# Seven unread matrix products fewer ahead of one k-v product, and GpSimd's gain product in two halves

## The chip, the core and the metric

The kernel runs on one core of one Trainium2 chip. The core has five engines with a queue each: PE (TensorE, matrix products; PEld is its weight load), DVE (VectorE), ACT (ScalarE), POOL (GpSimd) and SP (SyncE, which here only issues DMAs). The metric is the device time of one execution in microseconds (us); lower is better.

## The reference

There are eight batches, eight heads, 576 positions of 64 channels each. For each batch and head `kv = k^T v` (64x64), then `raw = q kv`, and each row of `raw` is divided by its root mean square and multiplied by `g_norm`. The heads side by side give `x`, 576x512 for each batch. Then

```
theta = x @ w_theta
y = w_tok_r @ (x * cos(theta)) + w_tok_i @ (x * sin(theta))    # mixes the 576 positions
u = x + y
out = u + max(u @ w_ch, 0)
```

## The kernel before, in words

**Tiling.** A batch's 576 positions are four tiles of 128 rows (j = 0 to 3, 512 columns: "full") and one rest of 64 rows, kept as a 128x256 tile (j = 4; its names carry an "e"). `g_norm` is folded into the weights, so the kernel's `x` and `u` are without it, and it comes back at the end as `ug = u * g`.

**The stages of a tile**, with the lines of the profile: `kv` on PE (L244, fp32, 80 small products a batch, copied to `kbd`); q turned, by PE in the first two batches and by DMA transposes from batch 2 on (L296); `raw` on PE (L309, L318); its squares on ACT (L331), their sums on DVE (L340), the power -1/2 on POOL (`rt`, L347), `x` on DVE (L372, L381); `x` turned by PE (L264) and copied out by ACT (`xT`, L280); `th` on PE (L402, L407); its whole turns (`pt`, ACT L420), the rest (`arg`, DVE L426) and its absolute value (DVE L434); sine and cosine (ACT L442, L449); `zm`, x times both (DVE L462; `zf` for the rest tile, which SP then moves to `zt` in four DMAs, L470); `y` on PE (L485, L489); `u` (DVE L496); `u` turned (PE L264, ACT L280), `v` on PE (L402, L407); `ug = u * g` on POOL (L525); `ot = max(v, 0) + ug` (DVE L535); the store (SP, L544, L549).

**Loads.** k and v of a batch (`kt`, `vt`, two buffers) are loaded by SP (L185, L189), q by POOL (L195, L202). `w_ch` is loaded once, by SP (L632), and scaled by ACT into `wch` (four instructions, L565).

**What sets the order.** Nothing is scheduled by the machine. Tasks are numbered as they are made, and a list in the source, `TURNS`, written out by hand, gives the order in which they are issued; each engine takes its own in that order and waits in place where an input is missing. An entry `~n@ring` is no task: it takes a slot of a PSUM ring (`acc` has 4, `raw` 2) and issues n products of the identity with a tile of ones into it (`idle`, L589, 128x512 fp16). Nothing reads them; they only fill PE's time. There are 64 such products, all in the first 40 us. `~9@acc` stands directly ahead of the k-v product of batch 1, which is 80 products (L244).

**POOL's queue** holds, besides the q loads, the 36 `rt` and the 40 `ug`. `ug` has two buffers for full tiles and two for rest tiles.

Of the kernel before, what the change touches and what calls it, by code (L numbers as in the profile page):

```python
# [13 lines left out]
ALU = mybir.AluOpType  # L14
# [24 lines left out]
44 120 38 47 129 104 121 105 107 130 39 ~2@acc 122 111 42 138 40 48 123 131 139 124 41 171 132 53  # L39
125 140 172 126 49 133 127 147 167 134 50 148 128 135 112 ~2@acc 181 51 141 168 113 149 136 142 52  # L40
182 183 115 114 54 150 156 184 144 143 ~1@acc 179 55 151 157 145 173 180 56 250 177 146 174 158 116
178 137 175 159 57 169 176 160 117 161 162 163 170 118 164 152 153 165 ~9@acc 255 119 154 256 251
# [70 lines left out]
def kernel(  # L113
# [12 lines left out]
    nc = tc.nc  # L126
    B, H, S, D = q.shape
    C = H * D
    P = 128
# [44 lines left out]
    g8 = const.tile([P, D], FP32, name="g8")  # L174
# [19 lines left out]
    def load_q(b, hs):  # L194
        nc.gpsimd.dma_start(  # L195
            out=qh[b % NB][:, hs, :],
            in_=q[b, hs, 0:SM, :].rearrange("h (p j) d -> p h (j d)", j=NJ),
        )

    def load_qe(b):  # L200
        for hh in range(2):
            nc.gpsimd.dma_start(  # L202
                out=qe[b % NB][hh * TL:(hh + 1) * TL, :, :],
                in_=q[b, hh * HH:(hh + 1) * HH, SM:S, :].rearrange("h s d -> s h d"),
            )
# [24 lines left out]
    def full(j):  # L230
        return j < NJ

    raw_ps, th_ps, y_ps, v_ps, kv_ps, tr_ps = {}, {}, {}, {}, {}, {}
    qT, x_sb, x_pair, sq_sb, rt_sb, xT, pt_sb, arg_sb, sc_sb, zf_sb, u_sb, ug_sb, uT, ot_sb = (
        {}, {}, {}, {}, {}, {}, {}, {}, {}, {}, {}, {}, {}, {})
# [286 lines left out]
    def u_gain(b, j):  # L522
        h, w, e = (H, C, "") if full(j) else (HH, HC, "e")
        ug = work.tile([P, w], FP32, tag="ug" + e, bufs=2, name="ug")
        nc.gpsimd.tensor_tensor(  # L525
            out=ug[:].rearrange("p (h e) -> p h e", h=h),
            in0=u_sb[b, j][:].rearrange("p (h e) -> p h e", h=h),
            in1=g8[:].unsqueeze(1).broadcast_to((P, h, D)), op=ALU.mult,
        )
        ug_sb[b, j] = ug  # L530

    def finish(b, j):
# [64 lines left out]
    def add(kind, eng, cost, fn, deps=(), pos=0.0, takes=(), tail=0.0, shape=None):  # L597
        t = Task(kind, eng, cost, fn, [d for d in deps if d is not None], pos,
                 [ring(*r) for r in takes], tail + (0.06 if eng == "PE" else 0.0), shape)
        tasks.append(t)  # L600
        return t
# [18 lines left out]
    def load(queue, cost, mbytes, fn, deps=(), pos=0.0, kind="load"):  # L620
        return transfer(kind, queue, cost, mbytes * MB, fn, deps, pos)
# [15 lines left out]
    pool, h = load("POOL", 1.0, 0.52, lambda: load_q(0, slice(0, HH)), [pool], -50)  # L637
    q_got[0, 0] = [h]
    pool, h = load("POOL", 1.0, 0.52, lambda: load_q(0, slice(HH, H)), [pool], -47.5)
    q_got[0, 1] = [h]  # L640
    pool, h = load("POOL", 1.3, 0.14, lambda: load_qe(0), [pool], -46)
# [44 lines left out]
    for kc in range(NKC):  # L686
        e = "DVE" if kc % 2 else "ACT"
# [14 lines left out]
    for b in range(B):  # L702
# [22 lines left out]
        for j in (0, 2, 1, 3, 4) if b == 0 else range(NT):  # L725
# [4 lines left out]
            if b < QD:  # L730
# [3 lines left out]
                e = "ACT" if b or a else "DVE"  # L734
# [79 lines left out]
        for j in range(NT):  # L814
# [28 lines left out]
            else:  # L843
# [7 lines left out]
                     [uo, *channel_ready], s, [PS_ACC], shape=sh)  # L851
            held_u.readers = [vv]
            ug = add("ug", "POOL", 1.16 if full(j) else 0.7, lambda b=b, j=j: u_gain(b, j), [um], s,
                     [("ug" + w, 2)])
            fin = add("fin", "DVE", 0.6 * f, lambda b=b, j=j: finish(b, j), [vv, ug], s,
# [53 lines left out]
```

## Time and profile before

| | |
|---|---|
| time, 3 runs | 222.99 us median (222.65 to 223.37) |
| the profiled execution | 223.69 us, of which 221.9 us span (first to last instruction) and 1.8 us around it |
| busy, share of the span | PE 207.4 us (93%), DVE 168.1 (76%), ACT 145.2 (65%), POOL 119.3 (54%) |
| granted TensorE clock | mean 0.988 |
| `idle` products (L589) | 64, 18.0 us busy |
| k-v products (L244) | 640, 22.2 us busy |
| `ug` (L525) | 40: 32 of 128x512 at 1186 ns mean, 8 of 128x256 at 674 ns mean |
| `rt` (L347) | 36, 55.0 us busy |
| `zm` (L462) | 32, 25.0 us busy, 789 ns mean |

How to read it: "busy" is the time in which an engine worked; PE's products overlap, so its busy share is high even where they are not dense. A row of the timeline is: start, length, engine, line, operation, what it writes and reads, shape, count, and in brackets the engine's idle time before it with what ended it. The chain of waits goes back from the last instruction, at each step to what released it; a piece called "issue" is time for which the profile names no releaser. "To landing" is the time from a DMA's issue until its data are there.

### The profile page before, as it was taken

To read this page: it belongs to the slowest core of one execution; us is meant where nothing else is said; L and a number is where in the kernel's file an instruction comes from. 1 tells how busy PE (TensorE), PEld (TensorE's weight loads), DVE (VectorE), ACT (ScalarE), POOL (GpSimd) and SP (SyncE) were. 2 spreads that over 40 slices of the span, in tenths; PEclk is the share of its full clock that TensorE was granted. 3 is DMA by queue.
4 is the path that set the end of the run, shared out by engine and by line. 5 is a ranking of instruction groups with operands and counts; after the bars stand their busy time and mean duration, and the time that the engine had idled before them with its cause. 6 is when DMAs were issued, how large, how long until landed. Compare 5 with 4: busy or idle time off the path is not lost.

```text
span 221.9 us, 5308 instructions
## 1 busy us (share of the span) xinstructions
PE 207.4 (93%) x2086; PEld 123.1 (55%) x2086; DVE 168.1 (76%) x314; ACT 145.2 (65%) x296; POOL 119.3 (54%) x113
## 2 busy tenths in 40 slices
PE   7599979999999999999999998999998999989991
PEld 2265545755855585557644764576556745444560
DVE  6027777279969799896998968988887797996651
ACT  2025997669992798668775894689538965674310
POOL 6031027088538885385876457872955358542360
PEclk9969999999999999999999999999999999999998
DMA  6999989999969998898969989979899216123044
GB/s 190 245 291 183 267 222 121 131 338 271 162 121 260 241 218 162 238 275 133 210 88 279 237 112 301 273 160 162 224 289 182 64 32 197 61 95 118 17 153 143
DMA packets 63291, 41.42 MB, mean 187 GB/s; under 512 B 29346, under 2 KB 58146, under 8 KB 63266
## 3 DMA queue, kind: packets, MB, share of 16 engines
q1 hardware_dynamic: 47762, 33.86, 59.5%
q0 software_dynamic: 13904, 6.05, 23.6%
q10 hardware_dynamic: 1600, 1.18, 1.7%
q8 instruction: 16, 0.26, 0.5%
q14 instruction: 9, 0.07, 0.1%
HBM read 33.10 MB, written 9.44 MB: 192 GB/s over the span
## 4 chain that ended last, share of the span: by engine, by line
PE 57%; DMA 18%; DVE 11%; ACT 5%; SPq 4%; issue 3%; POOL 0%; DVEq 0%; POOLq 0%; ACTq 0%
PE y L485 15%; DMA vt<-in_v_dram 10%; PE kv L244 8%; PE v L402 8%; PE th L402 7%; DMA qh<-in_q_dram 4%; DMA zt<-zf 4%; PE idle L589 3%; SPq L470 3%; PE y L489 3%; PE xps L264 3%; DVE arg L426 2%; PE ups L264 2%; DVE zm L462 2%; PE raw L309 2%
## 5 line engine op out<-in xcount | busy, mean ns | idle before, releaser
L347 POOL TENSOR_TENSOR rt<-ss,mhalf 128x8 f32<-128x8 f32 (+1 forms) x36 | 55.0, 1534 | 53.8 <-DVE ss L340 53.7
L485 PE MATMUL y<-zm,wT 128*128 128x512 f16 x256 | 65.3, 379 | 0.1
L525 POOL TENSOR_TENSOR ug<-u,g 128x512 f32<-128x512 f16 (+1 forms) x40 | 42.9, 1083 | 31.7 <-DVE ot L535 21.2
L485 PEld LDWEIGHTS <-wT 128*128 128x128 f16 x288 | 26.6, 98 | 28.1 <-issue 1.4
L402 PE MATMUL v<-wch,uT 128*128 128x512 f16 x128 | 32.5, 379 | 0.7 <-ACT uT L280 0.7
L402 PE MATMUL th<-wth,xT 128*128 128x512 f16 x128 | 32.4, 379 | 0.2 <-DVE ot L535 0.2
L426 DVE SCALAR_TENSOR_TENSOR arg<-pt,th 128x512 f32<-128x512 f32 (+1 forms) x40 | 25.0, 629 | 6.6 <-ACT pt L420 6.0
L331 ACT ACTIVATE sqb<-raw 128x512 f32<-128x512 f32 x32 | 19.0, 600 | 16.5 <-PE raw L309 16.4
L280 ACT COPY uT<-ups 128x512 f16<-128x512 f16 (+1 forms) x40 | 21.4, 543 | 12.1 <-PE ups L264 12.1
L420 ACT ACTIVATE pt<-th 128x512 f32<-128x512 f32 (+1 forms) x40 | 22.0, 555 | 9.8 <-PE th L402 9.3
L496 DVE TENSOR_TENSOR u<-y,x 128x512 f16<-128x512 f32 (+1 forms) x40 | 24.6, 631 | 5.0 <-PE y L485 3.7
L535 DVE SCALAR_TENSOR_TENSOR ot<-v,ug 128x512 f32<-128x512 f32 (+1 forms) x40 | 24.9, 630 | 4.7 <-PE v L402 4.5
L449 ACT ACTIVATE sc<-arg,quarter 128x512 f16<-128x512 f32 (+1 forms) x40 | 26.7, 675 | 2.3 <-DVE arg L434 2.1
L462 DVE TENSOR_TENSOR zm<-x,sc 128x1024 f16<-128x1024 f16 x32 | 25.0, 789 | 3.8 <-ACT sc L449 3.5
L340 DVE TENSOR_REDUCE ss<-sqb 128x8 f32<-128x520 f32 x32 | 21.9, 688 | 7.7 <-ACT sqb L331 7.5
L442 ACT ACTIVATE sc<-arg 128x512 f16<-128x512 f32 (+1 forms) x40 | 23.4, 587 | 5.2 <-DVE arg L426 5.1
L372 DVE TENSOR_TENSOR x<-raw,rt 128x512 f16<-128x512 f32 x32 | 21.8, 685 | 2.7 <-POOL rt L347 2.0
L280 ACT COPY xT<-xps 128x512 f16<-128x512 f16 (+1 forms) x40 | 20.8, 545 | 4.6 <-PE xps L264 4.5
L244 PE MATMUL kv<-vt,kt 128*64 128x64 f32 x640 | 22.2, 229 | 1.2 <-DMA vt<-in_v_dram 1.2
L244 PEld LDWEIGHTS kv<-vt,kt 128*64 128x64 f32 x640 | 21.0, 144 | 2.5 <-issue 2.1
L280 ACT CAST kbd<-kv 64x256 f16<-64x256 f32 (+1 forms) x30 | 10.5, 350 | 16.2 <-PE kv L244 15.8
L589 PE MATMUL idle<-fill,ident 128*128 128x512 f16 x64 | 18.0, 420 | 1.5 <-DVE fill L868 1.5
(73 smaller groups left out, 244.4 us busy)
## 6 DMA issues: line engine op xcount, KB each, us to landing
out_dram<-ot SPq DMA_DIRECT2D x32, 256.0 KB, 2.7
kt<-in_k_dram SPq DMA_DIRECT2D x7, 1024.0 KB, 7.7
vt<-in_v_dram SPq DMA_DIRECT2D x7, 1024.0 KB, 10.3
qh<-in_q_dram POOLq DMA_DIRECT2D x7, 512.0 KB, 7.2
kt<-in_k_dram SPq DMA_DIRECT2D x2, 512.0 KB, 6.7
vt<-in_v_dram ACTq DMA_DIRECT2D x2, 512.0 KB, 8.6
zm<-in_moe_w_theta_dram SPq DMA_DIRECT2D x1, 1024.0 KB, 13.9
zt<-zf SPq DMA_DIRECT2D x32, 32.0 KB, 2.4
```

Source lines behind the costliest of these rows:

```text
L244: nc.tensor.matmul(t[i * D:(i + 1) * D, hp - lo, :], kt[b % NKV][:, 2 * hp + i, j, :], vt[b % NKV][:, 2 * hp + i, j, :], start=(j == 0), s ...
L280: nc.scalar.copy(out=dst, in_=src)
L347: nc.gpsimd.tensor_tensor(out=rt[:], in0=ss[:], in1=mhalf[:, 0:h], op=ALU.pow)
L402: nc.tensor.matmul(t[:], lhs[:, kc, :], w[:, kc, :], start=first, stop=last)
L426: nc.vector.scalar_tensor_tensor(out=arg[:, 0, :], in0=pt_sb.pop((b, j))[:], scalar=MAGIC, in1=th_ps.pop((b, j))[:], op0=ALU.subtract, op1 ...
L449: nc.scalar.activation(out=sc_sb[b, j][:, 1, :], in_=arg_sb.pop((b, j))[:, 1, :], func=AFT.Sin, bias=quarter[:], scale=-TURN * SHRINK,)
L462: nc.vector.tensor_tensor(out=dst, in0=x.unsqueeze(1).broadcast_to((P, 2, w)), in1=sc[:], op=ALU.mult)
L485: nc.tensor.matmul(t[:], wT[:, w, j * P:(j + 1) * P], r, start=first, stop=last)
L496: nc.vector.tensor_tensor(out=u[:], in0=y_ps.pop((b, j))[:], in1=x_sb.pop((b, j)), op=ALU.add)
L525: nc.gpsimd.tensor_tensor(out=ug[:].rearrange("p (h e) -> p h e", h=h), in0=u_sb[b, j][:].rearrange("p (h e) -> p h e", h=h), in1=g8[:].un ...
L535: nc.vector.scalar_tensor_tensor(out=ot[:], in0=v_ps.pop((b, j))[:], scalar=0.0, in1=ug_sb.pop((b, j))[:], op0=ALU.max, op1=ALU.add,)
L589: nc.tensor.matmul(t[:], ident[:], fill[:], start=True, stop=True)
```

## The change

Two places are edited. In `TURNS`, `~9@acc` ahead of batch 1's k-v product becomes `~2@acc`; every other entry and the order stay as they were. In `u_gain` the one POOL product becomes two, over the first and the second half of the heads: two 128x256 for a full tile, two 128x128 for a rest tile. The program's order on every engine is otherwise the same.

```
-178 137 175 159 57 169 176 160 117 161 162 163 170 118 164 152 153 165 ~9@acc 255 119 154 256 251
+178 137 175 159 57 169 176 160 117 161 162 163 170 118 164 152 153 165 ~2@acc 255 119 154 256 251
...
     def u_gain(b, j):
         h, w, e = (H, C, "") if full(j) else (HH, HC, "e")
         ug = work.tile([P, w], FP32, tag="ug" + e, bufs=2, name="ug")
-        nc.gpsimd.tensor_tensor(
-            out=ug[:].rearrange("p (h e) -> p h e", h=h),
-            in0=u_sb[b, j][:].rearrange("p (h e) -> p h e", h=h),
-            in1=g8[:].unsqueeze(1).broadcast_to((P, h, D)), op=ALU.mult,
-        )
+        n = h // 2
+        for lo in (0, n):
+            cols = slice(lo * D, (lo + n) * D)
+            nc.gpsimd.tensor_tensor(
+                out=ug[:, cols].rearrange("p (h e) -> p h e", h=n),
+                in0=u_sb[b, j][:, cols].rearrange("p (h e) -> p h e", h=n),
+                in1=g8[:].unsqueeze(1).broadcast_to((P, n, D)), op=ALU.mult,
+            )
         ug_sb[b, j] = ug
```

## The prediction

> **What bounds the kernel now.** I read the chain of waits first, then PE's timeline around the edited turn, then the landing of the loads, then DVE beside POOL. The chain, around the edit:
>
> ```profile
> 36.90 0.35 PE wps L578 x4
> 37.25 0.15 PE wps L579
> 37.40 2.05 PE idle L589 x9
> 39.45 2.48 PE kv L244 x80
> 41.93 0.75 PE y L485 x3
> ```
>
> The nine unread products are themselves a link of the chain: the k-v product is released by PE's own queue and by nothing else, and from there the chain stays on PE to 83 us. So PE bounds this stage, and the nine are work in it. Were the k-v product's inputs there earlier? The view of tile vt, between 20 and 40 us, says how long its two loads (issued at 23.5 and 24.2 us) took:
>
> ```profile
> DMA to landing us min/median/max: 9.4/9.6/9.8
> ```
>
> They were there at 33.6 us, 5.8 us before the product at 39.4; kt, issued earlier, by 30.5. The end of the program is different: there the chain runs on DVE. DVE's and POOL's timelines:
>
> ```profile
> 189.56 0.69 DVE L426 SCALAR_TENSOR_TENSOR arg<-pt,th 128x512 f32<-128x512 f32 x1 [0.26 <-ACT pt L420]
> 190.28 1.47 DVE L434 TENSOR_SCALAR arg<-arg 128x512 int32<-128x512 int32 x1
> ...
> 194.51 1.27 DVE L462 TENSOR_TENSOR zm<-x,sc 128x1024 f16<-128x1024 f16 x1
> 195.71 0.68 DVE L496 TENSOR_TENSOR u<-y,x 128x512 f16<-128x512 f32 x1
> 196.31 1.05 DVE L462 TENSOR_TENSOR zm<-x,sc 128x1024 f16<-128x1024 f16 x1
> ...
> 200.68 1.20 DVE L462 TENSOR_TENSOR zm<-x,sc 128x1024 f16<-128x1024 f16 x1
> ```
> ```profile
> 188.54 2.92 POOL L525 TENSOR_TENSOR ug<-u,g 128x256 f32<-128x256 f16 x3
> 194.07 2.74 POOL L525 TENSOR_TENSOR ug<-u,g 128x512 f32<-128x512 f16 x2 [2.61 <-DVE ot L535]
> 200.17 1.16 POOL L525 TENSOR_TENSOR ug<-u,g 128x512 f32<-128x512 f16 x1 [3.36 <-DVE ot L535]
> ```
>
> An undisturbed zm takes 0.69 us, an undisturbed L434 0.42. The four long ones all begin while an ug runs, and all end a fixed time after that ug ends: 0.55 us for zm (200.17 + 1.16 = 201.33, zm's end is 201.88), 0.29 for L434. So while ug runs, these two DVE forms stand still. The view of line L462 shows the same over the whole run:
>
> ```profile
> L462 DVE TENSOR_TENSOR zm<-x,sc x32: 677/690/1719, 30.5 to 203.6; 128x1024 f16<-128x1024 f16 x32
> ```
>
> With a mean of 789 ns that is 32 x 0.10 = 3.2 us lost to it, in seven places (81.0, 98.9, 122.5, 127.2, 194.5, 196.3, 200.7 us), and 1.05 us in the one L434. A zm beside an rt (L347), the other long POOL form, keeps its 0.68: rt does not hold it.
>
> **Part 1: seven unread products fewer.** One costs PE's pitch: 18 dense y products take 3.88 us in the chain, 0.216 each. Seven are 1.51 us, all on the path, since the loads have 5.8 us in hand, batch 1's q (landed by 39.2 us, used at 42.5) would now be used at 41.0, and the k-v product's PSUM slot was freed by an arg that ended at 34.9. What is late next is the load of w_ch: issued by SP at 41.57, behind a DMA queue that nothing here moves, and 7.0 us to landing, so there at 48.57. ACT wants it at 49.44:
>
> ```profile
> 48.94 0.60 ACT L331 ACTIVATE sqb<-raw 128x512 f32<-128x512 f32 x1 [0.88 <-PE raw L309]
> 49.44 1.32 ACT L565 ACTIVATE wch<-zm,gcol 128x512 f16<-128x512 f32 x2
> 50.66 0.59 ACT L331 ACTIVATE sqb<-raw 128x512 f32<-128x512 f32 x1
> 51.14 1.07 ACT L280 COPY xT<-xps 128x512 f16<-128x512 f16 x2
> ```
>
> So ACT can come forward by 0.87 us and no more, and behind that wait stand the two sqb, xT and all else of ACT up to 60 us (it has no idle time there). PE's th at 52.00 needs the first xT, which ended at 51.72: 0.28 in hand. PE comes forward by 0.87 + 0.28 = 1.15; with a small pinch at 57 us (DVE's x for the last xps) I take 1.1. The bounds: 0.85 (if ACT's lead rules everywhere) and 1.51 (if its slack is larger than I see). The k-v product of batch 2 (57.99) would come to 56.9; its loads, not moved, land at 56.5. Later loads hang on zf and on kv themselves and move along. **Term: -1.1.**
>
> **Part 2: ug in two halves, the cost.** Start to start in POOL's queue a 128x512 takes 1.13 us and a 128x256, which the trace has as the rest tile's form, 0.63; two are 1.26, so +0.13 for each of 32. A 128x128 is not in the trace. Two of them lie between 0.63 (nothing added) and 1.26; on the line through the two rows one is 0.38, so +0.13 again, for 8. In all 40 x 0.13 = 5.2 us of POOL's time. Almost all of it is covered: every ug is ready 1.2 to 24 us before its ot (the smallest 1.18, at 214.8). What can be late is an rt straight behind an ug, since DVE's x takes some rt within 0.03 us of their end. That is the case at 88.39 (one ug ahead: +0.13, and DVE has 0.44 idle soon after) and at 160.65 (three ugs ahead: +0.4, in front of the wait for vt at 168.9, PE's own stall there being 0.58). The q loads in POOL's queue land 2.6 us or more before SP turns them. I take **+0.1**, bounds 0 and +0.5.
>
> The Trainium skill (Perfetto Trace Analysis, GPSIMD Engine Instruction) says that a GpSimd instruction's reported span should not be trusted and start-to-start spacing be used. By the spans (1.16 and 0.67) the split would cost 0.18 each and 7.2 us in all, by the spacing 0.13 and 5.2; under this cover both give the same term.
>
> **Part 2, the gain.** The DVE form waits for the rest of the ug; with halves it waits for the rest of one half, if it gets in between them. Two rows say that it does: at 194.07 two ugs stand back to back, zm (begun 194.51) runs when the first ends at 195.24, and the second, 1.62 us long instead of 1.16, waits for it; the same at 97.5, where an L434 goes ahead of a second ug. A third says that it need not: at 190.28 an L434 begun 0.06 us before the first ug's end waited for the second too. Case by case, with a half ending 0.5 us before the whole, and 0.13 later where the wait fell in the second half:
> - 81.04: 0.5 saved, on DVE's path to zf (83.6), whose four DMAs and two stores stand ahead of the loads of k and v of batch 4 in SP's queue. PE stalls for exactly those loads at 100.18, so they come 0.5 earlier, if the DMAs take as long. I take -0.4.
> - 122.49 saves 0.5, 127.18 loses 0.13, on the way to a zf whose DMA took 5.2 us behind other traffic. I take 0, bounds 0 and -0.4.
> - 190.28 to 200.68: 0.5 (or 1.0), 0.5, 0.3 and 0.5 of DVE time. PE's own stalls there (a product's start after the last one's, less the usual pitch) are 0.59 + 0.21 + 0.88 + 0.23 + 0.17 = 2.1 us, at 192.4, 194.7, 198.7, 201.9 and 202.5; behind them PE runs dense to the end, so what they lose is gained at the end. The phases will differ when all this runs an us or two earlier, so I take less than half: -0.8, bounds 0 and -2.0.
>
> **Sum:** -1.1 + 0.1 - 0.4 - 0.8 = -2.2 us. The profiled execution was 223.69 (221.9 + 1.8), so 221.5 for its like; the three runs' median lies 0.70 below it, and the same step from 222.99 gives 220.8. From bounds: -0.85 + 0.5 = -0.35 and -1.51 - 0.5 - 0.4 - 2.0 = -4.4.
>
> **Rivals.**
> - *The second half wins every time.* If POOL's second half takes its turn ahead of the waiting DVE form, as the second ug did at 190.28, the split gives nothing and costs its 0.1: -1.0, 222.0. Two rows of three speak against. The Trainium skill (SBUF — State Buffer, SBUF: two separate sides) calls this an exclusive lock that the first to start holds for its whole instruction; it does not say who is next when both wait, so it leaves this rival open.
> - *The time comes back as waits.* The w_ch load lands later than before, or batch 2's loads do (only 0.4 us would be in hand), and PE's lead shrinks to 0.3 by 60 us; with little from the split, 222.6. For it: both transfers are anchored in time, and DMA is busy through the whole stretch. Against: both were issued and landed with nothing of this change ahead of them.
> - *Slower: a zt move falls behind a burst.* The four small zt DMAs took from 1.8 to 5.2 us to landing, by what stood in the DMA queues; PE stalled for two of them (0.32 and 0.94 us at 115.6 and 137.9). If the new phases put one or two more behind k and v loads or transposes, each costs up to 5.2 - 1.8 = 3.4 us less PE's slack; it decides from about 2.2 us of new stall. Then 223.8 to 225. Against: almost all issues hang on the same compute and move together.
> - *Slower: the clock.* At the start PE stood idle from 8.5 to 10.9 us, and the granted clock was 0.50 in the stretch 12 to 15 us. If the seven products kept the clock up, 3.4 us at half clock cost 1.7 us, more than the 1.51 saved: 223.2 at least. Against: no hole opens, since the k-v product follows at once. The Trainium skill (TensorE: Matmul & The Clock Gate, Part 1) puts the fall at an idle window of some 3.4 us; by it nothing happens here. The trace's fall came after a hole of 2.4 us, so the measured hole is the one to beware of.
>
> **How the numbers follow.** The forecast 0.60 (220.8; its own range 219.6 to 221.8); the second half winning 0.18 (222.0); waits 0.11 (222.6); a late zt 0.09 (224); the clock 0.02 (223.5). 0.3% of 222.99 is 0.67 us, about what the measurement can tell. Faster by more: 0.60 + 0.18 = 0.78; within: 0.11; slower: 0.11. The range 219.6 to 222.7 leaves out the two slow cases, part of the waits and the best end of the bounds, some 2 in 10.
>
> **What would show it.** Right: kv of batch 1 starting near 37.9 us, without a gap; ACT idle some 0.6 us before the first wch; th of about 52.0 at 50.9; long zm of at most 1.3 us and PE's stalls of 190 to 203 us clearly under 2.1; 64 ug of 128x256 near 0.67 us. Wrong: zm still lasting to the end of the second half; kv of batch 2 waiting for vt; a granted clock below 1 around 40 us; new PE waits on zt.

## The result, and the profile after

| | before | after |
|---|---|---|
| time, 4 runs each, taken together | 223.18 us median (222.65 to 223.72) | 219.94 us median (219.70 to 221.20) |
| the profiled execution | 223.69 us, 221.9 us of it span | 219.70 us, 217.9 us of it span |
| busy, PE / DVE / ACT / POOL | 207.4 / 168.1 / 145.2 / 119.3 us | 204.5 / 165.6 / 145.4 / 127.4 us |
| `zm`, mean and longest | 789, 1719 ns | 744, 1193 ns |
| `arg` L434, longest | 1468 ns | 810 ns |

The ratio of the times is 0.9866, with a 95% interval of 0.9821 to 0.9912: 3.0 us faster (2.0 to 4.0). 220.8 had been forecast, 2.2 us faster. Times here and below are medians of all runs, while a ratio leaves out the slow ones (over 1.5% above the fastest of their kernel, among them one of five in q6_early and in q6_zero and the profiled runs of s_uneven and no_ug). From L525 on, the line numbers of after are up to 3 higher: `ug` is L528, `ot` L538, `idle` L592, `wch` L568.

**The edited turn.** The chain of waits of after, at the same place (start, length, engine, what):

```profile
36.35 0.35 PE wps L581 x4
36.85 0.54 PE idle L592 x2
37.39 2.48 PE kv L244 x80
39.87 0.75 PE y L485 x3
```

`idle` is now two products, and the k-v product starts 2.06 us earlier than in the first profile of before (39.45), with no wait of its own. Only 1.5 of the 2.06 are the edit's; the rest was there at the start of this execution (the table below). The landing of `vt` between 20 and 40 us:

```profile
DMA to landing us min/median/max: 10.1/10.3/10.6
```

They are slower than the 9.4 to 9.8 of before, but were issued at 23.3 and 24.1 us and so in place by 34.1, 3.2 us ahead of their use. ACT's timeline of after shows the load of `w_ch` as the next thing that is late:

```profile
46.88 0.60 ACT L331 ACTIVATE sqb<-raw 128x512 f32<-128x512 f32 x1 [0.88 <-PE raw L309]
47.71 1.33 ACT L568 ACTIVATE wch<-zm,gcol 128x512 f16<-128x512 f32 x2 [0.23 <-DMA zm<-in_moe_w_ch_dram]
48.95 0.58 ACT L331 ACTIVATE sqb<-raw 128x512 f32<-128x512 f32 x1
49.43 1.06 ACT L280 COPY xT<-xps 128x512 f16<-128x512 f16 x2
```

The first `wch` waits 0.23 us (0.6 had been expected), and `xT` behind it moved with it.

**The stretch before the end.** DVE's timeline of after, the rows that answer to L434 at 190.28 and `zm` at 194.51, 196.31 and 200.68, and then POOL's:

```profile
187.40 0.63 DVE L434 TENSOR_SCALAR arg<-arg 128x512 int32<-128x512 int32 x1
...
190.80 0.78 DVE L462 TENSOR_TENSOR zm<-x,sc 128x1024 f16<-128x1024 f16 x1
191.51 0.68 DVE L496 TENSOR_TENSOR u<-y,x 128x512 f16<-128x512 f32 x1
192.11 1.19 DVE L462 TENSOR_TENSOR zm<-x,sc 128x1024 f16<-128x1024 f16 x1
...
196.62 0.71 DVE L462 TENSOR_TENSOR zm<-x,sc 128x1024 f16<-128x1024 f16 x1
```
```profile
185.66 3.54 POOL L528 TENSOR_TENSOR ug<-u,g 128x128 f32<-128x128 f16 x6
190.36 3.47 POOL L528 TENSOR_TENSOR ug<-u,g 128x256 f32<-128x256 f16 x4 [1.17 <-DVE ot L538]
196.11 1.75 POOL L528 TENSOR_TENSOR ug<-u,g 128x256 f32<-128x256 f16 x2 [2.28 <-DVE ot L538]
```

The L434 came down from 1.47 to 0.63 us, the three `zm` from 1.27, 1.05 and 1.20 to 0.78, 1.19 and 0.71: together 1.68 us less (0.84 + 0.49 - 0.14 + 0.49). At 190.80 four half products stand back to back in POOL's queue, and `zm` ends at 191.58, 0.55 us after the first half and in front of the three others. The next `zm` fares worse: it begins at 192.11, as the second half ends (192.12), and ends at 193.30, 0.55 us after the third (192.75). So it waits for a whole half, and takes longer than before. The first POOL row holds six: two halves of a rest tile, whose form it shows, and four of full tiles.

PE's own stalls here, 2.1 us before, are 0.20 at 191.21 (`th`) and 0.35 at 194.61 (`v`): 0.55 in all. Over the whole run the view of line L462 gives, and that of tile `ug`:

```profile
L462 DVE TENSOR_TENSOR zm<-x,sc x32: 678/686/1193, 30.0 to 199.1; 128x1024 f16<-128x1024 f16 x32
```
```profile
L528 POOL TENSOR_TENSOR ug<-u,g x80: 421/673/1127, 47.0 to 211.4; 128x256 f32<-128x256 f16 x64, 128x128 f32<-128x128 f16 x16
```

The longest `zm` lost half a microsecond, and the rest tile's new 128x128 form takes 0.42 us by its span (0.39 from start to start; 0.38 was the estimate).

**What got worse** is one wait in the chain of after:

```profile
129.88 5.87 DMA zt<-zf
135.79 0.38 PE y L485
```

PE stalls 1.68 us here for the last `zt` move of batch 4 (the fifth batch; the first is 0), 1.10 before (a product's start after the last one's, less the usual pitch; the prediction's 0.94 for it is PE's idle time alone).

**Where the time came from.** PE carries the same products in all kernels (but for `idle`), so the trace gives a lead: how much earlier a product starts than its like in the first profile of before. The table shows by how much the lead grew in each stretch, in us; the marks are times of before. The first column is the lead at 18.27 us, which no edit touches.

```
                 start  18-39   39-58   58-84   84-169  169-end   18-end
                        filler  w_ch    zm, b2  loads   zm, end
before_again      2.20  -0.05    0.00    0.00    0.77    0.00      0.72
after             0.56   1.50   -0.20    0.35    0.65    1.60      3.90
after_again       1.67   1.50    0.01    0.36   -0.45    1.62      3.03
f_only           -0.25   1.46   -0.78   -0.01    1.11   -0.12      1.66
s_only            2.11  -0.06    0.00    0.36    1.50    1.62      3.42
f_sixteen         0.88  -1.58    0.00    0.03    0.67    0.02     -0.86
s_uneven          0.25   1.46   -0.01   -0.06   -0.62    0.12      0.89
s_quarters        0.18   1.51   -0.05    0.22    0.65    1.00      3.33
no_ug            -2.15   1.49   -0.33   -0.07    3.05    0.52      4.66
f_wch_early       1.85   1.49    0.01    0.04    1.25   -1.01      1.78
both_early        1.50   1.51    0.00    0.06    1.64    0.83      4.04
q6_early          1.12   1.51    0.00    0.36    2.88    1.61      6.36
q6_zero           1.67   2.04   -0.86    0.36    2.92    1.61      6.07
```

Three columns are made by the edits and repeat to a few hundredths wherever the same edit stands and no wait for a k-v load falls into the column: the filler, the `zm` of batch 2 and the `zm` at the end. Such waits shift some entries. In the third column, s_uneven and both_early gain 0.36 at `th` (83.75) and lose 0.37 and 0.24 at the k-v product of 78.2. At the last mark, the wait for the k-v loads of batch 7 lies just ahead of it in before and just behind it in f_wch_early, both_early and no_ug (0.97, 0.75 and 1.43 us), so it counts as a gain in the column of the loads and as a loss in the last one. Two columns are not made by the edits: the start, which differs by 4.3 us between executions, and the stretch of the loads, in which two profiles of one kernel differ by 0.8 (before) and 1.1 us (after). So single times of one kernel spread over 1.5 to 4.7 us, and the medians have the intervals given with each ratio.

### The profile page after: what moved, and what is told of

Same layout as the page of the kernel before. It is cut to its first block, busy times and chain, and to the rows that moved or that the text cites. A ratio compares the mean times of both kernels' runs of the same rounds, so it can differ in the third digit from the quotient of the medians.

```text
span 217.9 us, 5336 instructions
## 1 busy us (share of the span) xinstructions
PE 204.5 (94%) x2079; PEld 121.0 (56%) x2079; DVE 165.6 (76%) x314; ACT 145.4 (67%) x296; POOL 127.4 (58%) x153
## 4 chain that ended last, share of the span: by engine, by line
PE 65%; DMA 14%; DVE 9%; ACT 5%; SPq 3%; issue 2%; POOL 0%; DVEq 0%; POOLq 0%; ACTq 0%
PE y L485 20%; PE v L402 9%; PE th L402 9%; PE kv L244 8%; DMA zt<-zf 5%; DMA qh<-in_q_dram 4%; DMA vt<-in_v_dram 4%; PE xps L264 3%; PE y L489 3%; PE ups L264 3%; PE raw L309 2%; PE idle L592 2%; DVE arg L426 2%; SPq L470 2%; DVE ot L538 2%
## 5 line engine op out<-in xcount | busy, mean ns | idle before, releaser
L528 POOL TENSOR_TENSOR ug<-u,g 128x256 f32<-128x256 f16 (+1 forms) x80 | 51.0, 663 | 24.4 <-DVE ot L538 15.4
L538 DVE SCALAR_TENSOR_TENSOR ot<-v,ug 128x512 f32<-128x512 f32 (+1 forms) x40 | 25.0, 631 | 3.8 <-PE v L402 3.7
L462 DVE TENSOR_TENSOR zm<-x,sc 128x1024 f16<-128x1024 f16 x32 | 23.6, 744 | 4.0 <-ACT sc L449 3.9
L442 ACT ACTIVATE sc<-arg 128x512 f16<-128x512 f32 (+1 forms) x40 | 23.3, 587 | 3.8 <-DVE arg L426 3.7
L244 PE MATMUL kv<-vt,kt 128*64 128x64 f32 x640 | 21.0, 223 | 0.2 <-DMA vt<-in_v_dram 0.2
L244 PEld LDWEIGHTS kv<-vt,kt 128*64 128x64 f32 x640 | 19.9, 138 | 1.4 <-issue 0.9
L592 PE MATMUL idle<-fill,ident 128*128 128x512 f16 x57 | 16.7, 430 | 1.5 <-DVE fill L871 1.5
```

Of the source, the lines that this page charges most:

```text
L244: nc.tensor.matmul(t[i * D:(i + 1) * D, hp - lo, :], kt[b % NKV][:, 2 * hp + i, j, :], vt[b % NKV][:, 2 * hp + i, j, :], start=(j == 0), s ...
L442: nc.scalar.activation(out=sc[:, 0, :], in_=arg_sb[b, j][:, 0, :], func=AFT.Sin, bias=0.0, scale=-TURN * SHRINK,)
L462: nc.vector.tensor_tensor(out=dst, in0=x.unsqueeze(1).broadcast_to((P, 2, w)), in1=sc[:], op=ALU.mult)
L528: nc.gpsimd.tensor_tensor(out=ug[:, cols].rearrange("p (h e) -> p h e", h=n), in0=u_sb[b, j][:, cols].rearrange("p (h e) -> p h e", h=n), ...
L538: nc.vector.scalar_tensor_tensor(out=ot[:], in0=v_ps.pop((b, j))[:], scalar=0.0, in1=ug_sb.pop((b, j))[:], op0=ALU.max, op1=ALU.add,)
```

## The experiments

"Theory" is that the products are work on PE's path, and that one `ug` holds DVE's `zm` and L434 for its whole length, so that halves shorten the hold. The rivals are those of the prediction.

**f_only and s_only: each part alone.** f_only has `~2@acc` and the whole `ug`; s_only has the two halves and `~9@acc`.

```
-... 152 153 165 ~9@acc 255 119 154 256 251
+... 152 153 165 ~2@acc 255 119 154 256 251
```

> Two instead of nine unread products, ug whole. Theory (two separate gains: PE work removed, and shorter holds of DVE by ug): about 1.1 to 1.4 us under the kernel before, so a ratio near 0.994 to 0.995; PE's stalls at 192 to 203 us stay near 2 us and zm still reaches 1.2 us or more. Rival (all of the gain is the seven products, the split is a free rider): the whole 3 us, ratio 0.987. Rival (the filler's time comes back as waits and the gain is the split's): ratio 1.000.

> Nine unread products as before, ug in halves. Theory: 1.5 to 2 us under the kernel before, ratio 0.991 to 0.993; the longest zm near 1.2 us instead of 1.7, L434 never over 0.8, PE's stalls between 188 and 203 us about 1 us less. Rival (the seven products do it all): ratio 1.000. Rival (the filler's time comes back): 0.987, as the whole change.

Measured: f_only 221.24 against 222.61 us, ratio 0.9941 (0.9904 to 0.9979); s_only 219.39, 0.9879 (0.9818 to 0.9941). The first is as the theory had it, 1.3 us; the second is better than it had it. By time alone s_only is as fast as the whole change, as the rival "the filler's time comes back" has it; against that rival stand f_only's time (1.000 by the rival) and the table. The `zm` row of f_only and that of s_only:

```profile
L462 DVE TENSOR_TENSOR zm<-x,sc x32: 678/688/1715, 30.8 to 202.2; 128x1024 f16<-128x1024 f16 x32
```
```profile
L462 DVE TENSOR_TENSOR zm<-x,sc x32: 680/690/1185, 28.5 to 198.0; 128x1024 f16<-128x1024 f16 x32
```

The short hold goes with the halves alone. In the table the filler column is all f_only's and the two `zm` columns are all s_only's: in f_only the end gains nothing (PE's stalls there are 0.58, 0.21, 0.89, 0.24 and 0.17 us, as before), although all of it runs 1.4 us earlier. DVE's timeline of f_only has the same long rows as before, to a hundredth or two:

```profile
188.85 1.46 DVE L434 TENSOR_SCALAR arg<-arg 128x512 int32<-128x512 int32 x1
...
193.08 1.28 DVE L462 TENSOR_TENSOR zm<-x,sc 128x1024 f16<-128x1024 f16 x1
...
194.88 1.05 DVE L462 TENSOR_TENSOR zm<-x,sc 128x1024 f16<-128x1024 f16 x1
...
199.26 1.21 DVE L462 TENSOR_TENSOR zm<-x,sc 128x1024 f16<-128x1024 f16 x1
```

So an earlier arrival does not change how `ug` and `zm` meet. ACT's row at the `w_ch` load in f_only (landed at 49.04 us, in after at 47.60):

```profile
49.14 1.33 ACT L565 ACTIVATE wch<-zm,gcol 128x512 f16<-128x512 f32 x2 [0.81 <-DMA zm<-in_moe_w_ch_dram]
```

Here the load took back 0.78 of the 1.46 us. Whether the two parts add is not settled: the product of the ratios is 0.982, the ratio of both 0.9866 and 0.9851, and all the intervals overlap.

**s_uneven: one head and seven.** `~2@acc`, and two `ug` instructions as in after, but of unlike size: as many instructions, nearly the old hold.

```
-        for lo in (0, n):
+        for lo, n in ((0, 1), (1, h - 1)):
```

> Two unread products, ug in two parts again, but unequal: one head and the other seven (one and three in a rest tile). POOL pays the same for two instructions; the long part still holds DVE for about 1.0 us instead of 0.65. Theory (the longest single hold decides): most of the split's gain is lost, ratio 0.992 to 0.995, close to that of two products with ug whole. Rival (any second instruction does it, by moved phases or by letting DVE in once): ratio 0.987, as the whole change.

Measured: 220.67 against 222.61, 0.9921 (0.9882 to 0.9961), about f_only's time.

```profile
L462 DVE TENSOR_TENSOR zm<-x,sc x32: 680/690/1454, 30.3 to 202.5; 128x1024 f16<-128x1024 f16 x32
```

The longest `zm` is 1.45 us, and the end gains 0.12 us. Where `zm` gets in behind the short part it takes 0.80 us (at 79.77, 1.72 before), and PE gains 0.36 us there, as with halves. So what counts is the length of the one instruction that `zm` meets, not that there are two.

**s_quarters: four parts.** `~2@acc`, four `ug` of two heads each (of one for the rest tile).

```
-        n = h // 2
-        for lo in (0, n):
+        n = h // 4
+        for lo in range(0, h, n):
```

> Two unread products, ug in four parts. By the line through the rows of the two sizes a part takes 0.38 us of POOL start to start, so a full ug takes 1.5 instead of 1.26. Theory: holds of at most 0.4 us, waits shorter by a further 0.1 to 0.2 us each, POOL 8 to 10 us busier; 0.2 to 0.6 us under the changed kernel, ratio 0.984 to 0.987. Rival (POOL's added time reaches x through rt): 0.5 to 1 us over the changed kernel, ratio 0.989 to 0.991.

Measured: 220.37 against 222.61, 0.9879 (0.9808 to 0.9951), between what theory and rival had and not to be told from the halves. DVE's timeline of s_quarters at the end:

```profile
191.95 0.93 DVE L462 TENSOR_TENSOR zm<-x,sc 128x1024 f16<-128x1024 f16 x1
...
193.40 0.70 DVE L462 TENSOR_TENSOR zm<-x,sc 128x1024 f16<-128x1024 f16 x1
...
197.50 0.86 DVE L462 TENSOR_TENSOR zm<-x,sc 128x1024 f16<-128x1024 f16 x1
```

The longest `zm` is down to 0.93 us, yet the end gains 1.00 instead of 1.60: PE still stalls 0.67 us at 195.41. And it stalls 0.41 us at 90.03 and 0.34 at 164.02, for an `x` whose `rt` stands behind an `ug`: just after the two places (88.39, 160.65) that the prediction had named for the cost of part 2. With halves PE has no stall there.

**no_ug: no `ug` at all.** `~2@acc`; `ot` reads a tile of zeros, so that the kernel computes max(u w_ch, 0) without the u*g that is added to it. It tells what `ug` costs as a whole.

```
+    none = const.tile([P, C], FP32, name="none")
...
-            nc.gpsimd.tensor_tensor(
...
-        ug_sb[b, j] = ug
+        ug_sb[b, j] = none[:, 0:C if full(j) else HC]
...
+        nc.vector.memset(none[:], 0.0)
```

> Two unread products, and the product u * g left out: ot adds a tile of zeros instead, POOL has no ug at all. The output is max(v, 0). This is the most that a shorter hold can give. Theory (ug holds DVE): no zm over 0.75 us, no L434 over 0.5; 0.3 to 1.0 us under the changed kernel, ratio 0.982 to 0.985, since halves already took most of it off PE's path. Rival (what the halves gave came from elsewhere): long zm remain, beside rt.

Measured: 218.85 against 222.16, 0.9833 (0.9765 to 0.9901): not to be told from after on the same chip (0.9851), so halves already have what can be seen of it. In its profile each of the 32 `zm` takes its own time, as the theory says; L434 has one exception, which it had not foreseen:

```profile
L463 DVE TENSOR_TENSOR zm<-x,sc x32: 680/686/694, 32.7 to 200.8; 128x1024 f16<-128x1024 f16 x32
```
```profile
79.45 1.19 DVE L435 TENSOR_SCALAR arg<-arg 128x512 int32<-128x512 int32 x2
```
```profile
79.48 0.94 POOL L196 DMA_DIRECT2D qh<-in_q_dram  x1
```

Two L434 (L435 here) in a row, of which the second began at 79.80 and took 0.84 us instead of 0.42. It ended at 80.64, 0.22 us after POOL had finished issuing a q load (80.42). Nothing else ran on POOL. This longer L434 may be why no_ug lacks the 0.35 us that the halves gain in the third column; that is argued, not shown. In this profile the granted clock was low at the start and PE waited 1.43 us for the last k-v loads, so its columns of start, loads and end are no measure of `ug`.

**f_sixteen: seven more instead of seven fewer.** `~16@acc`, whole `ug`.

> Sixteen instead of nine unread products, ug whole: seven more, the change's first part in reverse. Theory (they are work on PE's path, with nothing beside them to hide in): 7 x 0.216 = 1.5 us later at the k-v product of batch 1, and 1.0 to 1.6 us over the kernel before at the end, ratio 1.005 to 1.007. Rival (the early lead or delay is swallowed by later waits for DMA): under 0.5 us, ratio 1.000 to 1.002.

Measured: 223.76 against 222.16, 1.0085 (1.0043 to 1.0127), 1.6 to 1.9 us slower, at or a little over the theory's upper end. Its chain:

```profile
36.60 3.56 PE idle L589 x16
40.16 2.48 PE kv L244 x80
```

The lead falls by 1.58, of which 1.51 comes between the product ahead of the seven and the k-v product, and up to 84 us nothing takes it back. So upward each product costs 1.51 / 7 = 0.216 us. The same price both ways shows that they are work on the path and not a cover for a wait.

**f_wch_early: is the `w_ch` load what caps part 1?** f_only with that load (task 58) issued some 14 us earlier, behind task 53.

```
-... 41 171 132 53
+... 41 171 132 53 58
...
-257 252 258 58 196 166 259 ...
+257 252 258 196 166 259 ...
```

> Two unread products, ug whole, and the load of w_ch issued by SP right behind the loads of batch 1, some 13 us before its old place. With ug whole and the load in its old place ACT waited 0.8 us for w_ch and PE stalled 0.7 us at 51.5 us. Theory (that wait takes back part of the lead): no wait of ACT for w_ch, PE's lead at th equal to that at the k-v product within 0.1 us, ratio 0.990 to 0.993. Rival (the lead is lost later anyway): 0.994 to 0.995, as without this edit. Against both: the earlier load delays batch 1's vt past 37 us, and the k-v product waits.

ACT's row shows that the wait is gone, and the lead stays whole (1.49, then 0.01):

```profile
46.09 1.32 ACT L565 ACTIVATE wch<-zm,gcol 128x512 f16<-128x512 f32 x2
```

But the time is not better: 221.18 against 221.20, 1.0008 (0.9970 to 1.0046). That is neither what the theory had nor what the rival had. The one profile does not show why: its stalls further on (0.53 and 0.92 us at `zt`, 0.97 for the k-v loads of batch 7) stand where before has stalls too (0.48, 1.10 and 0.75), and the 1.01 that the end column loses is the last of them, counted behind the mark. The cap exists, but issuing `w_ch` earlier won nothing that could be measured; why is open.

**before_again and after_again: the same kernels once more**, to see which waits belong to the kernel.

> The kernel before once more, for a second profile. In the first one PE stalled 0.75 us at the k-v product of batch 7, whose vt took 11.1 us to landing; in the profiles with seven products fewer and with seven more, both with ug whole, it did not stall there. Theory (a chance of DMA, no part of what the change won): the stall is under 0.3 us here, vt lands in about 10 us, and the stalls at 192 to 203 us are the same as in the first profile, within 0.2 us. Rival (the stall belongs to the kernel before): 0.6 us or more again.

> The changed kernel once more, beside the three others on the same chip. The seven products alone gave a ratio of 0.994 and the halves alone 0.988; if the two added up, both together would give 0.982. Theory (they don't add: what PE gains early is partly given back where it waits for a zt that lands with the q load ahead of it): 0.985 to 0.988. Rival (they add, and the first comparison of the changed kernel fell on slow starts): 0.980 to 0.983.

after_again: 218.24 against 222.16, 0.9851 (0.9785 to 0.9917). before_again: one run, 220.79 (span 219.0). Its stalls at the end are those of before (0.58, 0.21, 0.89, 0.23, 0.17). Its stall for `zt` of batch 4 is 1.60 (1.10 before), that for the k-v loads of batch 7 is 0.51 (0.75 before), between the two values that would have decided. So the end repeats exactly, and the DMA waits do not: the stall for `zt` is 1.10 and 1.60 in two profiles of before, 1.68 and 1.86 in two of after. In the two kernels with one part alone it is 1.23 (f_only) and 0.88 (s_only), so that the change makes this stall longer is not shown.

**q6_early: what does `zt` of batch 4 wait for?** (The expectation counts it as 5.) After, with POOL's q load of batch 6 (task 882) issued behind task 666, ahead of one `ug`, some 5 us earlier.

```
-... 769 797 693 666 791 723 ...
+... 769 797 693 666 882 791 723 ...
...
-... 810 680 703 882 796 812 532
+... 810 680 703 796 812 532
```

> The changed kernel with the q load of batch 6 issued one ug earlier in POOL's queue, some 3 us before its old place. In the changed kernel the zt of batch 5 lands at 135.8 us, together with the last piece of that q load (136.0), and PE stalls 1.7 us for it. Theory (zt stands behind that q load): zt lands 2 to 3 us earlier, the stall falls under 0.5 us, and the time falls by 0.5 to 1.5 us against the changed kernel: ratio 0.979 to 0.984. Rival (the total of DMA traffic sets it, whatever the order): zt lands within 0.5 us of before, the same time as the changed kernel.

Measured: 218.09 against 222.16, 0.9787 (0.9724 to 0.9850). POOL's timeline of after, and then of q6_early:

```profile
124.70 0.98 POOL L195 DMA_DIRECT2D qh<-in_q_dram  x1
125.68 1.25 POOL L202 DMA_DIRECT2D qe<-in_q_dram  x2
```
```profile
119.86 1.07 POOL L195 DMA_DIRECT2D qh<-in_q_dram  x1
120.93 1.26 POOL L202 DMA_DIRECT2D qe<-in_q_dram  x2
```

The `zt` moves themselves are issued earlier too in q6_early (125.32 to 128.10) than in after (126.80 to 130.53), since `zf` is ready 1.49 us sooner in that execution (125.28, 126.77). The view of tile `zt` in this window gives their time to landing, in after and in q6_early:

```profile
DMA to landing us min/median/max: 5.9/7.2/8.4
```
```profile
DMA to landing us min/median/max: 4.4/5.5/6.1
```

The last one lands at 131.95 instead of 135.75, and PE's stall is gone; the chain of q6_early passes the place on PE:

```profile
131.87 1.29 PE y L485 x6
133.16 0.22 PE raw L309 x4
133.38 0.65 PE y L485 x3
```

In after the q load landed at 135.95, just behind the moves; in q6_early at 128.74, ahead of them. Only the load's place differs between the two kernels. To leave out the earlier `zf`, take the time from the end of `zf` to the landing of the last move:

```
                                                     load issued     zf end to last     PE's stall
                                                     ahead of zf     zt landing         for zt
ten profiles with the load in its old place          0.8 to 2.1      8.06 to 9.25       0.88 to 1.86
q6_early, q6_zero, both_early                        5.4             6.61 to 6.78       none
no_ug (no ug ahead of the load in POOL's queue)      7.3             4.94               none
```

So the load's place is worth some 1.3 to 2.6 us to the moves, and this wait can be removed. It is not all that the moves are late behind: in f_wch_early the load landed at 131.01, 2.8 us ahead of the last move, which still came 8.10 us after `zf`, and the quickest move of before took 1.8 us. By time q6_early (0.9787) and after_again (0.9851) are not to be told apart, since their intervals overlap; by the lead, q6_early is ahead.

**both_early and q6_zero: what the findings suggest together.** both_early is q6_early with the early `w_ch` load; q6_zero is q6_early with `~0@acc`.

> The changed kernel with the load of w_ch issued early and the q load of batch 6 issued one ug earlier. With the q load alone the ratio was 0.979. Theory: the w_ch wait is small with this kernel (0 to 0.2 us), so 0.977 to 0.979. Rival (the earlier load delays batch 1's vt): 0.980 or more.

> The changed kernel with the q load of batch 6 issued one ug earlier, and none instead of two unread products. Theory (each is 0.216 us of PE's path until the next late input): another 0.2 to 0.4 us, ratio 0.977 to 0.978, if the k-v product's inputs and w_ch allow it. Rival (the w_ch load takes it all): 0.979, as with two.

Measured against 221.20: both_early 218.83, 0.9879 (0.9826 to 0.9932); q6_zero 217.02, 0.9798 (0.9730 to 0.9866). With the early `w_ch` PE stalls 1.36 and 0.74 us for the k-v loads of batches 4 and 7; after_again has 1.41 for the first without it, so these do not show that the early load costs anything. Without the last two products the filler column rises by 0.53 to 2.04, and the load takes 0.86 back:

```profile
46.73 1.33 ACT L568 ACTIVATE wch<-zm,gcol 128x512 f16<-128x512 f32 x2 [0.68 <-DMA zm<-in_moe_w_ch_dram]
```

q6_zero and q6_early have the lowest ratios, and are not to be told apart.

## Why the prediction was right, and where it was not

The direction was right, so were the places of the two large gains, and the time lies in the range. The sum was too small (-2.2, measured -3.0 with 2.0 to 4.0), by one term above all, and one smaller term came out by another path than forecast.

- **The seven products, 0.216 each on the path: right.** The lead grew by 1.46 to 1.51 us in each of the eight kernels with two products (seven times 0.216 is 1.51), and fell by 1.58 with sixteen, 1.51 of it at the k-v product.
- **The cap by `w_ch`, net -1.1: the mechanism right, the size a matter of the execution.** The load took back 0.20 (after), gave 0.01 (after_again) and took back 0.78 (f_only). Net that is 1.30, 1.51 and 0.68 against 1.1, and 1.3 by the time of f_only alone; that 1.1 lies in the middle of these is luck. As the prediction said, the seven products do not move the load's issue: it came 0.55 us earlier than before in after and 1.66 in after_again, which is the lead that both had at the start (0.56, 1.67). What varied is the time to landing, taken as 7.0: it was 6.6 in after, 6.3 in after_again and 7.2 in f_only, in the order of what they lost. Each lost about what its landing took over 6.4 us, by which 7.0 would have left 0.9 and not 1.1. The 0.28 us in hand at `th` was too much: it was read at the first product (52.00), but the weight load is what reads `xT`, and in before it stands at 51.79, 0.07 us after `xT`'s end:

```profile
51.79 0.75 PEld L402 LDWEIGHTS <-xT 128*128 128x128 f16 x4
```

- **The cost of the halves, +0.1: too small to see.** POOL has 8.1 us more of span (7.2 by the spans had been worked out), and no stall of PE at the two places named. With quarters it is there, 0.41 and 0.34 us. The bound below (0) was nearer for halves.
- **`zm` ahead of `zf` (batch 2), -0.4: the size right by luck, the path wrong.** The two `zm` at 81.04 together took 2.32 us before and 2.32 in f_only, 1.76 in after, and PE's lead grew by 0.35 or 0.36 in each kernel with halves that had no other stall ahead of it. But it grew at the product `th` at 83.75, and not where the term had put it, at the k-v product of batch 4 (100.18). In before PE waits there (0.20 us of idle time) for an `ot` of DVE that stands right behind the two `zm`; in after that wait is gone. The pages of before and after:

```profile
L402 PE MATMUL th<-wth,xT 128*128 128x512 f16 x128 | 32.4, 379 | 0.2 <-DVE ot L535 0.2
L402 PE MATMUL th<-wth,xT 128*128 128x512 f16 x128 | 32.4, 380 | 0.0
```

  Whether the k and v loads of batch 4 also come forward can't be read: PE's stall for them was 0.79 and none in two profiles of before, 0.33 and 1.41 in two of after.
- **0 at 122.5 and 127.2 us: not contradicted.** What is lost or won there is hidden by the wait for `zt`. (The prediction gave the `zt` moves 1.8 to 5.2 us to landing; the view of before goes to 7.3, and 5.2 is the last of batch 4's four.)
- **The end, -0.8: the step that was mis-sized.** It measured -1.60, -1.62, -1.62, -1.61 and -1.61 in the five kernels with halves and no new stall in this stretch. I had worked out 2.1 us of stalls and then taken less than half, because "the phases will differ when all this runs an us or two earlier". They do not: f_only runs 1.4 us earlier and has the same five stalls to 0.01 us. The rows fit this: the later `ug` groups wait for a free buffer, that is for DVE's own `ot` ("<-DVE ot" in brackets), and the first stands right behind an `rt` that DVE's `ss` releases (in f_only as in after). POOL's start hangs on DVE, so both move together. That this is the reason is read from the rows, not tested by a run of its own. The step itself was already there, case by case (0.5 or 1.0, 0.5, 0.3, 0.5 of DVE time; measured 0.84, 0.49, -0.14, 0.49), and only the discount was without ground. The prediction also counted "the one L434" as held; before has a second, 0.95 us at 146.08 beside an `ug`, and after has none over 0.5 there.
- **The rivals.** That the second half always wins: no, but it can. DVE's `zm` at 190.80 and L434 at 187.40 (ended 188.03, 0.29 us after the first half's end at 187.74) both got in between halves, and the `zm` at 192.11 did not. That the time comes back as waits: in part, 0.78 us at the `w_ch` load in f_only; the loads of batch 2 were in time (in after they landed at 55.65, and the k-v product began at 56.13). The Trainium skill (SBUF — State Buffer, SBUF: two separate sides) describes an exclusive lock held for a whole instruction; the trace agrees for `ug`, since the 0.55 us after an instruction's end stay and only the instruction became shorter. The `zt` move behind a burst: in part; one such stall was 0.1 to 0.8 us longer than in before's profiles, not the 2.2 that would have decided. The clock: no, it was 1.00 from 30 to 50 us.

## What to carry to other kernels

Ask what starts each of two instructions that collide: where one is released by the other's engine, a shift of all that lies ahead need not change how they collide (here the stalls stayed the same to 0.01 us), and the gain from shortening the hold needs no discount for it. Products that only fill time are free while an input is late and cost their full length from then on, so compare the landing of the inputs with their use. A load anchored in time caps a gain ahead of it, and whether issuing it earlier helps has to be measured: here one such move gave nothing, and another removed a stall. A slack in front of a product is read at its weight load, if that is what reads the late tile.

## What the runs showed of the hardware

- **`ug` holds `zm`, `rt` does not.** Nine of the 32 `zm` of after began while an `rt` of 1.0 to 2.0 us ran, and none took over 0.69 us. The Trainium skill (SBUF — State Buffer, SBUF: two separate sides) has a DVE operation with two SBUF inputs held by any GpSimd operation that reads SBUF; `rt` reads two small SBUF tiles (128x8), and here the measurement decides: not by this one.
- **A DMA issue on POOL goes with a longer DVE instruction, too.** L434 took 0.84 instead of 0.42 us beside a q load's issue (no_ug, begun 0.32 us into the issue), and its 128x256 form 0.54 instead of 0.28 (before, 128.03, begun 0.53 us into one). A 128x512 L434 that began in the first 0.27 us of an issue kept its 0.42 (before, 78.86).
- **The clock at the start.** PE has nothing but `idle` until the first q lands (9.3 to 11.3 us). In three profiles its idle time before that was 2.30, 2.41 and 2.76 us (s_quarters, before, no_ug) and the granted clock fell to 0.50 between 12 and 15 us; in the others it was 2.06 or less and the clock stayed at 1.00 there. The Trainium skill (TensorE: Matmul & The Clock Gate, Part 1) puts the fall at an idle window of some 3.4 us; these rows have it from 2.3.
- **The start alone spreads the runs**: by 18 us, before any edit, PE's lead differs by 4.3 us between executions.
